# Folding w_phi in quarter-array tiles of 60 by 64

## The chip, the cores and the metric

The kernel runs on one core of one Trainium2 chip. The metric is the time of one execution on the device in microseconds (us); lower is better. The core has five engines with a queue each: TensorE (PE; its weight loads are shown as PEld), VectorE (DVE), ScalarE (ACT), GpSimd (POOL) and SyncE (SP), which issues the DMAs here. PE writes to PSUM banks only; DVE and ACT copy from there.

## The reference

Two layers, each a linear attention with a learned feature map and a dense block with Mish, both on layer-normed rows and added to their input. S = 2048 rows, D = 640, H = 32 heads of 20, F = 1536, all in float32.

```python
def A(x, wqkv, w_phi, wo):
    q, k, v = split(x @ wqkv)                       # B, H, S, 20 each
    pq, pk = q @ w_phi[h], k @ w_phi[h]             # per head, 20 by 20
    phi_q = concat(softmax(pq), softmax(-pq))
    phi_k = concat(softmax(pk), softmax(-pk))
    kv, z = phi_k.T @ v, sum over s of phi_k
    return ((phi_q @ kv) / (phi_q @ z + 1e-6)) @ wo
def B(x, w1, b1, w2): return mish(x @ w1 + b1) @ w2
for _ in range(2):
    x = x + A(layernorm(x), wqkv, w_phi, wo)
    x = x + B(layernorm(x), w1, b1, w2)
```

## The kernel before

**Numbers in two parts.** A matrix product of float32 precision is made of three fp32r products: high by high, high by low, low by high. A weight or an activation is therefore kept as a pair: `hi` is copied by ACT with rounding to fp32r, and `lo` is the difference, made by DVE or POOL. `split` (L141) does it for weights that lie in SBUF, `fold_end` (L272) for products in PSUM, and `Transposed.step` (L316) for transposed rows (`xth`, `xtl`).

**The fold.** Since the features depend on q and k only through q·w_phi and k·w_phi, the kernel multiplies w_phi into the weights of queries and keys once, at the start of the first layer. A softmax does not change when a constant is taken off each head's 20 scores, so one of the 20 columns is subtracted from the other 19 (`shift_phi`, on POOL) and DL = 19 columns a head are kept: 608 in all. The weights of queries and keys come transposed from DRAM (`wqk_t`), in six raw tiles for the queries and six for the keys (`load_raw`). `bd` holds w_phi as blocks along a diagonal: 120 rows, six tiles, 120 columns. `fold_part` multiplies raw tile t (up to 120 rows, six heads) by one of the five 128-column slices k, with f32 operands; an f32 product is recorded twice in the trace. A tile's result is up to 114 columns wide. Three tiles fill one PSUM bank, 342 or 266 columns, and `fold_end` evicts it: one ACT copy to `r2h` (queries) or `r1h` (keys), one DVE subtraction to `r2l` or `r1l`. There are ten evictions for the queries and ten for the keys.

**PSUM.** There are eight banks: two tiles `mm` of two banks each and four tiles `one` of one bank. A tile is handed out again only when its readers are done with it.

**The start.** Under `written()` the order of PE, SP, ACT, DVE and POOL is the order of the code. 30 transposes of the identity come first on PE. SP issues the first 256 rows of x (a block: two tiles of 128 rows), w_phi, the raw tiles of the queries, the values' weights, the raw tiles of the keys and the next block's rows, in this order. On PE follow the first fold (tiles 0 to 2) of slices 0 to 3, the ten transposes of the first block's normed rows `xn`, the first fold of slice 4, the first half of the first queries' projection (`project_half`: 15 products, three per slice), the second folds (tiles 3 to 5) of all five slices, and the second half. On ACT the eviction of slice 0 stands ahead of `xn[0]`. `make_v` splits the values' weights between the evictions of the second folds.

**The first layer's blocks.** Afterwards a scheduler orders PE, ACT, DVE and POOL by its own estimates of time; `tc.issue_after(x)` keeps an instruction behind x. Block 0 goes through `q0 v0 v1 k0 q1 k1`; the digit is the tile of 128 rows. The keys' fold (`fold_phi`) stands in the code ahead of `k0`. `features` turns projected queries or keys into softmax features: eviction by ACT, reduces and subtractions on DVE and POOL (L416 to L419), exp on ACT, a sum, a reciprocal and a product (L425 on DVE, L426 on DVE, L427 on POOL). For keys PE then accumulates the state `kva` (L464: 32 products of 21 by 40 columns a tile). For queries DVE transposes the features (L478) and SP writes them to DRAM in four pieces (`e_d`). `fetch_normed(b + 1)` makes the statistics of the next block: four `bn_stats` and two aggregates on DVE, a power on POOL.

**The rest.** `attend_second` makes the outputs of the attention; its `average` (L686) multiplies features by the state in products of 64 columns of the stationary operand, one for each half of PSUM's partitions. `dense` makes the second part of the layer. The second layer does the same with the folded weights from DRAM (`wp_d`).

## Time and profile before

| | |
|---|---|
| median of 3 runs | 1363.56 us (1362.27 to 1363.75) |
| the profiled execution's own time | 1361.69 us |
| its span, first to last instruction | 1359.7 us |
| busy PE, DVE, ACT, POOL | 1349.6, 1057.4, 576.0, 464.0 us |
| mean granted clock of PE | 0.999 |

The span is what the trace shows; the profiled execution's own time is 2.0 us more. In the rows of the trace a line such as L262 is the line of the kernel, `out<-in` are the names of the tiles that an instruction writes and reads, x is a count, and the text in brackets tells how long the engine was idle in front of it and what ended that. Matmuls are pipelined, so the rows of PE overlap: the distance of two starts is the price of a product, not its own length.

### The profile page before, as it was taken

How to read it: one execution, taken by the hardware profiler on the slowest of the kernel's cores; microseconds unless marked ns; L12 is line 12 of the kernel's file. 1: busy time of each engine (PE TensorE's matmuls, PEld its weight loads, DVE VectorE, ACT ScalarE, POOL GpSimd, SP SyncE). 2: the span in 40 equal slices, each digit the busy share in tenths (PEclk: the TensorE clock that was granted, in tenths of full speed). 3: DMA queues.
4: the chain of work that ended last, by engine and by line, in shares of the span. 5: the costliest groups of instructions: out<-in, count | busy, mean ns of one | idle time of the engine just before them, and what ended most of it. 6: DMA issues, size and time to landing. Idle time of an engine off the chain costs nothing.

```text
span 1359.7 us, 30969 instructions
## 1 busy us (share of the span) xinstructions
PE 1349.6 (99%) x12896; PEld 1338.2 (98%) x12896; DVE 1057.4 (78%) x1799; ACT 576.0 (42%) x967; POOL 464.0 (34%) x417
## 2 busy tenths in 40 slices
PE   9999999999999999999999999999999999999998
PEld 9999999999999999999999999999999999999998
DVE  5888988876687887778769788779668776676775
ACT  4444344322454545445443334332236444444443
POOL 2355644444222222222225555634351211111111
PEclk9999999999999999999999999999999999999999
DMA  9543443797714442244563534559964221233200
GB/s 338 156 103 79 98 96 81 206 287 274 222 40 98 117 117 69 61 106 100 145 209 81 119 79 91 96 120 289 289 246 125 78 72 39 86 98 97 73 26 20
DMA packets 352629, 174.11 MB, mean 128 GB/s; under 512 B 287449, under 2 KB 324041, under 8 KB 352489
## 3 DMA queue, kind: packets, MB, share of 16 engines
q1 hardware_dynamic: 352489, 172.14, 46.7%
q8 instruction: 101, 1.65, 0.5%
q14 instruction: 39, 0.32, 0.1%
HBM read 106.23 MB, written 65.86 MB: 127 GB/s over the span
## 4 chain that ended last, share of the span: by engine, by line
PE 94%; DVE 3%; POOL 1%; ACT 0%; issue 0%; DVEq 0%; POOLq 0%
PE mm L391 25%; PE mm L851 25%; PE one L809 25%; PE one L391 12%; PE mm L686 3%; PE one L325 2%; PE one L464 2%; DVE r L425 1%; DVE m L416 0%; DVE r L419 0%; POOL big L427 0%; DVE big L417 0%; DVE r1l L276 0%; POOL xtl L331 0%; POOL r L427 0%
## 5 line engine op out<-in xcount | busy, mean ns | idle before, releaser
L851 PE MATMUL mm<-r2h,ol 128*128 128x320 f32 x1280 | 304.8, 309 | 0.0
L835 POOL TENSOR_TENSOR ol<-big,ol 128x512 fp32r<-128x512 f32 (+1 forms) x98 | 131.1, 1338 | 477.2 <-ACT ol L834 419.1
L809 PE MATMUL one<-xtl,r1h 128*128 128x256 f32 x960 | 268.2, 279 | 0.0
L809 PE MATMUL one<-xth,r1l 128*128 128x256 f32 x960 | 268.0, 279 | 0.0
L809 PE MATMUL one<-xth,r1h 128*128 128x256 f32 x960 | 265.9, 279 | 0.0
L851 PEld LDWEIGHTS mm<-r2h,ol 128*128 128x128 f32 x1280 | 219.2, 188 | 0.0
L851 PE MATMUL mm<-r2l,ol 128*128 128x320 f32 x640 | 197.3, 309 | 0.0
L391 PE MATMUL mm<-r1h,xth 128*128 128x304 f32 (+1 forms) x600 | 185.1, 309 | 1.5 <-DVE r1l L276 1.5
L391 PE MATMUL mm<-r1l,xth 128*128 128x304 f32 (+1 forms) x600 | 183.8, 306 | 0.0
L391 PE MATMUL mm<-r1h,xtl 128*128 128x304 f32 (+1 forms) x600 | 183.5, 306 | 0.2 <-POOL xtl L331 0.2
L809 PEld LDWEIGHTS one<-xtl,r1h 128*128 128x128 f32 x960 | 180.4, 188 | 0.0
L809 PEld LDWEIGHTS one<-xth,r1l 128*128 128x128 f32 x960 | 180.4, 188 | 0.0
L809 PEld LDWEIGHTS one<-xth,r1h 128*128 128x128 f32 x960 | 179.6, 188 | 0.0
L824 DVE TENSOR_SCALAR big<-big 128x512 f32<-128x512 f32 (+1 forms) x98 | 56.6, 578 | 110.0 <-ACT big L822 109.8
L851 PEld LDWEIGHTS mm<-r2l,ol 128*128 128x128 f32 x640 | 120.2, 188 | 0.0
L834 ACT ACTIVATE ol<-big 128x512 fp32r<-128x512 f32 (+1 forms) x98 | 60.9, 622 | 137.8 <-DVE big L833 137.8
L826 ACT ACTIVATE big<-big,two 128x512 f32<-128x512 f32 (+1 forms) x98 | 70.1, 716 | 116.0 <-DVE big L825 115.9
L822 ACT ACTIVATE big<-one,b1s 128x256 f32<-128x256 f32 x192 | 80.9, 468 | 88.5 <-PE one L809 88.0
L427 POOL TENSOR_TENSOR r<-r,r 128x1280 f32<-128x1280 f32 x32 | 77.2, 2413 | 119.1 <-DVE r L426 101.6
L391 PEld LDWEIGHTS mm<-r1h,xth 128*128 128x128 f32 x600 | 112.8, 188 | 2.6 <-DVE r1l L276 1.7
L391 PEld LDWEIGHTS mm<-r1h,xtl 128*128 128x128 f32 x600 | 112.8, 188 | 0.4 <-POOL xtl L331 0.4
L391 PEld LDWEIGHTS mm<-r1l,xth 128*128 128x128 f32 x600 | 112.8, 188 | 0.1
(142 smaller groups left out, 3118.0 us busy)
## 6 DMA issues: line engine op xcount, KB each, us to landing
e_d<-r SPq DMA_DIRECT2D x128, 160.0 KB, 4.0
big<-e_d SPq DMA_DIRECT2D x32, 640.0 KB, 7.6
x_d<-xt SPq DMA_DIRECT2D x23, 640.0 KB, 3.8
xt<-x_d SPq DMA_DIRECT2D x22, 640.0 KB, 5.5
n_d<-xn SPq DMA_DIRECT2D x168, 80.0 KB, 2.3
xt<-in_x SPq DMA_DIRECT2D x16, 640.0 KB, 4.4
xn<-x_d SPq DMA_DIRECT2D x28, 320.0 KB, 4.4
v<-n_d SPq DMA_DIRECT2D x30, 256.0 KB, 3.1
```

The costliest lines, as they stand in the source:

```text
L325: nc.tensor.transpose(ps[:, c, t * P:(t + 1) * P], self.rows[t][:, (c0 + c) * P:(c0 + c + 1) * P], ident)
L391: nc.tensor.matmul(ps[:, :w], a[:, sl], r, start=(k == 0 and n == 0), stop=(k == KD - 1 and n == 2))
L427: nc.gpsimd.tensor_tensor(eg, eg, r.unsqueeze(2).to_broadcast([P, 2 * H, DH]), op=ALU.mult)
L464: nc.tensor.matmul(kva[32 * j:32 * j + DH + 1, 40 * r:40 * r + 40], v[:, (DH + 1) * h:(DH + 1) * (h + 1)], e[:, 40 * h:40 * h + 40], start ...
L686: nc.tensor.matmul(po[64 * q:64 * q + 64, c, GW * j:GW * j + w], phs[g][:n, s0:s0 + 64], kvb[:n, g, :w], start=True, stop=True)
L809: nc.tensor.matmul(ph[:, j, :], l, r, start=(n == 0), stop=(n == 3 * KD - 1))
L822: exps[0] = nc.scalar.activation(part(ta, 0)[:, j - js.start], ph[:, j, :], AF.Exp, bias=b1s[:, 2 * pr + j:2 * pr + j + 1]).ins
L824: nc.vector.tensor_scalar_min(e, e, E_CAP)
L826: nc.scalar.activation(r, n, AF.Ln, bias=two)
L834: nc.scalar.activation(ah[:, js], n, AF.Copy)
L835: nc.gpsimd.tensor_tensor(al[:, js], n, ah[:, js].bitcast(F32), op=ALU.subtract)
L851: nc.tensor.matmul(pys[t][:, c, :HC], l[:, j, sl], r, start=(f == 0 and n == 0), stop=(f == KF - 1 and n == 2))
```

## The change

Each group of the fold (one raw tile, one slice) is made of four products of 60 (or 64) rows by 64 columns of the raw tile, with 57 columns of w_phi, in place of one of up to 120 rows by 128 columns with 114. Rows 0 to 63 and rows 64 to 123 go to two PSUM banks, the two 64-column halves of a slice to the two halves of a bank's partitions. The sixth tile has only the upper rows: two products. So that a half starts at row 64, a raw tile is loaded from four rows further up, with those rows meeting zeros in `bd`; `bd` is now 128 rows by six tiles of 60 columns, filled with zeros by DVE first. `fold_end` evicts both banks of an `mm` tile in one instruction with a two-part pattern, and two `one` tiles in two instructions; the sixth tile's 38 columns of an `mm` tile take one more.

The order at the start changes too: the first fold begins with three slices, `xn[0]` on ACT and `xn[1]` on DVE stand ahead of all evictions, the folds of slices 3 and 4 follow between the transposes, the first half of the first queries' projection comes behind the second folds of slices 0 and 1, and `make_v` starts one slice later. The keys' fold is in two parts: slices 0 and 1 ahead of `v1`, slices 2 to 4 behind it and ahead of `k0`, each behind the product that PE was given last. The first queries' next steps (`advance`) go behind the last eviction of the keys' fold. The statistics are tied down: those of block 1 behind the last v split, of block 3 behind a reciprocal of block 1, of the others behind the last eviction of the fold.

```diff
         raw = []
         for t in ts:
-            rows = 120 if t < 4 else 80
-            if t < 5:
-                r = wts.tile([P, D], F32, tag=f"r2{'hl'[which]}{5 + t}", name=f"raw{which}{t}")
-            else:
-                r = r2_wide(10 + which, F32)[:, 0]
-
-            n = P if t < 5 else rows
-            c0 = which * D + (t * 120 if t < 5 else D - rows)
-            nc.sync.dma_start(r[:n], wqk_t[c0:c0 + n, :])
-            raw.append((r, rows))
+            r = (wts.tile([P, D], F32, tag=f"r2{'hl'[which]}{5 + t}", name=f"raw{which}{t}") if t < 5 else
+                 r2_wide(10 + which, F32)[:, 0])
+            p0 = 4 if which == t == 0 else 0
+            n = 124 if p0 else P if t < 5 else 64
+            c0 = which * D + (120 * t - 4 if t < 5 else D - 64)
+            if p0:
+                nc.vector.memset(r[:p0], 0.0)
+            nc.sync.dma_start(r[p0:n], wqk_t[c0 + p0:c0 + n, :])
+            raw.append(r)
         return raw
 
-    def fold_part(ps, k, t, bd, raw):
-
-        r, rows = raw[t]
-        heads = rows // DH
-        n = DL * (6 * (t % 3) if t < 5 else 10)
-        nc.tensor.matmul(ps[:, n:n + heads * DL].rearrange("p (j d) -> p j d", d=DL), r[:rows, k * P:(k + 1) * P],
-                         bd[:rows, t, :rows].rearrange("p (j d) -> p j d", d=DH)[:, :, :DL], start=True, stop=True)
+    def load_phi(bd):
+
+        nc.vector.memset(bd, 0.0)
+        for s in range(2):
+            nc.sync.dma_start(bd[4 + 60 * s:64 + 60 * s, :5], phi_bd[60 * s:60 * s + 60, :5, 60 * s:60 * s + 60])
+        nc.sync.dma_start(bd[24:64, 5, :40], phi_bd[:40, 5, :40])
 
...
-    def fold_end(ws, ps, k, c):
-        n0, n1 = (0, 18 * DL) if c == 0 else (18 * DL, QK)
-        hi, lo = ws[k][0][:, n0:n1], ws[k][1][:, n0:n1]
-        nc.scalar.activation(hi, ps[:, :n1 - n0], AF.Copy)
-        nc.vector.tensor_tensor(lo, ps[:, :n1 - n0], hi.bitcast(F32), op=ALU.subtract)
-
-    def fold_phi(ws, bd, raw):
-
-        pss = {}
-        for k, c in ((0, 0), (1, 0), (2, 0), (3, 0), (0, 1), (1, 1), (2, 1), (3, 1), (4, 0), (4, 1)):
-            if c == 0:
-                mm = None if k % 2 else mm_tile()
-                pss[k] = [one_tile(), one_tile()] if k % 2 else [mm[:, 0], mm[:, 1]]
-            ps = pss[k][c]
-            for t in range(3 * c, 3 * c + 3):
-                fold_part(ps, k, t, bd, raw)
-            fold_end(ws, ps, k, c)
+    def pair_banks(single):
+
+        if single:
+            return [one_tile(), one_tile()]
+        mm = mm_tile()
+        return [mm[:, 0], mm[:, 1], mm]
+
+    def fold_part(ps, k, t, t0, bd, raw):
+
+        n = 3 * (t - t0) * DL
+        heads = 3 if t < 5 or len(ps) == 2 else 2
+        for s in range(2 if t < 5 else 1):
+            rows = slice(64 * s, 64 if s == 0 else 124)
+            rhs = bd[rows, t, :heads * DH].rearrange("p (j d) -> p j d", d=DH)[:, :, :DL]
+            for q in range(2):
+                last_product[0] = nc.tensor.matmul(
+                    ps[s][64 * q:64 * q + 64, n:n + heads * DL].rearrange("p (j d) -> p j d", d=DL),
+                    raw[t][rows, k * P + 64 * q:k * P + 64 * q + 64], rhs, start=True, stop=True).ins
+
+    def fold_end(ws, ps, k, t0, t1):
+
+        n = min(t1, 5) - t0
+        w = 3 * DL
+        c0 = 2 * t0 * w
+
+        outs = []
+        if len(ps) > 2:
+            out = [x[:, c0:c0 + 2 * n * w].rearrange("p (t s d) -> p s t d", t=n, s=2) for x in ws[k]]
+            outs.append((ps[2][:, :, :n * w].rearrange("p s (t d) -> p s t d", t=n), *out))
+            if t1 > 5:
+                outs.append((ps[0][:, n * w:n * w + 2 * DL], *(x[:, 10 * w:QK] for x in ws[k])))
+        else:
+            for s in range(2):
+                m = t1 - t0 if s == 0 else n
+                out = [x[:, c0 + s * w:c0 + (2 * m - 1 + s) * w] for x in ws[k]]
+                out = [bass.AP(tensor=x.tensor, offset=x.offset, ap=[x.ap[0], [2 * w, m], [1, w]]) for x in out]
+                outs.append((ps[s][:, :m * w].rearrange("p (t d) -> p t d", t=m), *out))
+        for src, hi, lo in outs:
+            last_copy[0] = nc.scalar.activation(hi, src, AF.Copy).ins
+            last_fold[0] = nc.vector.tensor_tensor(lo, src, hi.bitcast(F32), op=ALU.subtract).ins
+
+    def fold_phi(ws, bd, raw, ks):
+
+        for k in ks:
+            ps = pair_banks(k == 3)
+            for t in range(6):
+                fold_part(ps, k, t, 0, bd, raw)
+            fold_end(ws, ps, k, 0, 6)
...
             xt = fetch(x_src, b) if b > 1 else early
-            norm_scale(b, [norm_stats(t, xt) for t in range(BT)])
+            with tc.issue_after(last_split[0] if b == 1 else early_recip[0] if b == 3 else last_fold[0]):
+                norm_scale(b, [norm_stats(t, xt) for t in range(BT)])
...
-                bd = big_tile()[:120, :720].rearrange("p (t c) -> p t c", t=6)
-                nc.sync.dma_start(bd[:, :3], phi_bd[:, :3])
+                bd = big_tile()[:, :360].rearrange("p (t c) -> p t c", t=6)
+                load_phi(bd)
...
-                shift_phi(bd, slice(3, 5))
-                shift_phi(bd, 5)
+                shift_phi(bd, slice(3, 6))
...
                 q_ws = [r2_pair(k) for k in range(KD)]
-                mm = [mm_tile(), mm_tile()]
-                pcs = [mm[0][:, 0], mm[0][:, 1], mm[1][:, 0], mm[1][:, 1], one_tile()]
+                def fold(ps, k, t0):
+                    for t in range(t0, t0 + 3):
+                        fold_part(ps, k, t, t0, bd, raw_q)
+
+                def make_v(k):
+                    split(kv_ws[k][0][:, D:2 * D], kv_ws[k][1][:, D:2 * D], raw_v[k])
+
+                pcs = [pair_banks(k == 2) for k in range(3)]
                 for t in range(3):
-                    for k in range(KD - 1):
-                        fold_part(pcs[k], k, t, bd, raw_q)
-                fold_end(q_ws, pcs[0], 0, 0)
+                    for k in range(3):
+                        fold_part(pcs[k], k, t, 0, bd, raw_q)
                 xn = [row_tile() for _ in range(BT)]
                 act(xn[0], xt[:, 0, :], AF.Identity, bias=stats[:, 0, 1, 0:1], scale=stats[:, 0, 0, 0:1])
                 nc.vector.tensor_scalar(xn[1], xt[:, 1, :], stats[:, 0, 0, 1:2], stats[:, 0, 1, 1:2],
                                         op0=ALU.mult, op1=ALU.add)
-                fold_end(q_ws, pcs[1], 1, 0)
-                fold_end(q_ws, pcs[2], 2, 0)
+                fold_end(q_ws, pcs[0], 0, 0, 3)
                 nxt = Transposed(xn)
                 nxt.step()
-                fold_end(q_ws, pcs[3], 3, 0)
+                pcs.append(pair_banks(False))
+                fold(pcs[3], 3, 0)
+                fold_end(q_ws, pcs[1], 1, 0, 3)
+                fold_end(q_ws, pcs[2], 2, 0, 3)
                 nxt.step()
-                for t in range(3):
-                    fold_part(pcs[4], 4, t, bd, raw_q)
+                pcs.append(pair_banks(True))
+                fold(pcs[4], 4, 0)
+                fold_end(q_ws, pcs[3], 3, 0, 3)
                 nxt.step()
-                fold_end(q_ws, pcs[4], 4, 0)
+                fold_end(q_ws, pcs[4], 4, 0, 3)
                 mm = mm_tile()
                 q0 = [mm[:, 0], mm[:, 1], mm]
-                project_half(q0[0], nxt, 0, q_ws, 0, 0, w=QC)
-
-                def make_v(k):
-                    split(kv_ws[k][0][:, D:2 * D], kv_ws[k][1][:, D:2 * D], raw_v[k])
-
                 for k in range(KD):
-                    ps = one_tile()
-                    for t in range(3, 6):
-                        fold_part(ps, k, t, bd, raw_q)
-                    fold_end(q_ws, ps, k, 1)
-                    if k > 0:
-                        make_v(k - 1)
+                    ps = pair_banks(k in (1, 2, 4))
+                    fold(ps, k, 3)
+                    fold_end(q_ws, ps, k, 3, 6)
+                    if k == 1:
+                        project_half(q0[0], nxt, 0, q_ws, 0, 0, w=QC)
+                    elif k > 1:
+                        make_v(k - 2)
                 project_half(q0[1], nxt, 0, q_ws, 0, 1, w=QC)
+                make_v(KD - 2)
                 make_v(KD - 1)
...
                 i = b * BT + t
+                if b == 0 and layer == 0 and n in (2, 3):
+                    with tc.issue_after(last_product[0]):
+                        fold_phi(kv_ws, bd, raw, range(2) if n == 2 else range(2, KD))
                 if b == 0 and n == (1 if layer else 3):
-                    if layer == 0:
-                        fold_phi(kv_ws, bd, raw)
...
-                if b == NB - 1 and n == 3:
+                if b == 0 and not layer:
+                    with tc.issue_after(last_product[0]):
+                        next(g)
+                    if n == 3:
+                        with tc.issue_after(last_fold[0]), tc.issue_after(last_copy[0]):
+                            advance()
+                    elif n != 2:
+                        advance()
...
+                if b == 1 and n == 0:
+                    early_recip[0] = last_recip[0]
```

21 lines of the change are left out of this document (9 added, 12 removed).

## The prediction

> **What bounds the kernel now.** I read the page first, then busy time by stretches, then the timeline of TensorE (PE) up to 43 us, then the groups of the first 43 us by shape.
>
> ```profile
> span 1359.7 us, 30969 instructions
> ...
> PE 1349.6 (99%) x12896; PEld 1338.2 (98%) x12896; DVE 1057.4 (78%) x1799; ACT 576.0 (42%) x967; POOL 464.0 (34%) x417
> ```
> ```profile
> 0.00:20.00 20.00, 17.75 (x127) 17.19 (x128) 10.00 (x27) 8.95 (x19) 3.76 (x16) 1.00 0.94 317
> 20.00:40.00 20.00, 17.46 (x133) 17.07 (x133) 16.20 (x41) 10.05 (x22) 6.56 (x9) 1.00 1.00 361
> 40.00:60.00 20.00, 20.00 (x147) 20.00 (x146) 15.23 (x26) 6.20 (x9) 3.97 (x8) 1.00 0.52 132
> 60.00:80.00 20.00, 20.00 (x260) 19.51 (x259) 19.99 (x26) 8.98 (x12) 10.06 (x7) 1.00 0.34 72
> 80.00:100.00 20.00, 20.00 (x257) 19.51 (x256) 15.79 (x22) 9.69 (x15) 12.48 (x13) 1.00 0.52 133
> ```
>
> After the stretch come its length and then the busy time of PE, PEld, DVE, ACT, POOL, the granted clock, the DMA share and GB/s. PE is the bound, and the 10 us in which it is idle (1359.7 less 1349.6) lie, as far as these stretches reach, in the first 40 us: 20 − 17.75 and 20 − 17.46. From 40 us on it has no gap. DVE is full from 60 to 80 us, though, so PE can be moved forward there only as far as DVE follows.
>
> The change touches only the work up to the first keys; the built programs' orders agree on every engine again from about the third block of rows on (near 100 us). So the question is how much earlier PE reaches its gapless part, and whether that part stays gapless.
>
> ```profile
> 1.15 0.47 SPq L503 DMA_DIRECT2D big<-in_phi_bd  x1
> 1.68 1.30 SPq L253 DMA_DIRECT2D raw<-in_wqk_t  x3
> ...
> 7.13 2.83 PE L262 MATMUL mm<-big,raw 120*128 120x114 f32 x24
> ...
> 8.12 0.23 DVE L307 SCALAR_TENSOR_TENSOR stats<-mv,stats 128x1 f32<-128x1 f32 x2 [1.10 <-POOL stats L305]
> ...
> 9.90 0.91 ACT L131 ACTIVATE xn<-xt,stats 128x640 f32<-128x640 f32 x1
> 10.87 1.25 PE L325 MATMUL one<-ident,xn 128*128 128x128 f32 x8 [0.91 <-ACT xn L131]
> 12.74 0.39 PE L391 MATMUL mm<-r2h,xth 128*128 128x304 f32 x1
> ...
> 30.15 0.82 PE L262 MATMUL one<-big,raw 120*128 120x114 f32 x6
> 30.80 0.83 PE L262 MATMUL mm<-big,raw 120*128 120x114 f32 x6
> ...
> 35.34 0.67 PE L262 MATMUL mm<-big,raw 120*128 120x114 f32 x4 [1.05 <-DVE r1l L276]
> 39.47 0.41 PE L391 MATMUL mm<-r1h,xth 128*128 128x304 f32 x1 [1.49 <-DVE r1l L276]
> ...
> 41.98 0.39 PE L391 MATMUL mm<-r1l,xth 128*128 128x304 f32 x1
> 42.20 0.31 PE L391 MATMUL mm<-r1h,xtl 128*128 128x304 f32 x1
> ```
>
> The columns are start, length, engine, line, operation and, in brackets, the idle time in front. Three gaps of PE stand here: 0.91 us, in which the transposes wait for the norm of the first rows, and 1.05 and 1.49 us, in which the keys' fold waits for DVE's evictions: 3.45 us. The last two rows end the first half of the first keys' projection (15 products) at 42.4 us. That is my checkpoint: both programs have then done the same PE work, all ten transposes of the second block included.
>
> **Term 1: the fold on PE.** I call a group one raw tile times one 128-column slice: 6 tiles × 5 slices × 2 (queries, keys) = 60. Before, a group is one product, recorded twice (f32). Three start at 30.15 and the next three at 30.80: 0.22 us a group, 13.2 us in all. After, a group is four products of 64 by 64 and 57 columns (two for the sixth tile), one in each quarter of the array. The trace has no products in row halves; it has them in column parts:
>
> ```profile
> 251.64 0.30 PE L391 MATMUL one<-r2l,xth 128*128 128x304 f32 x1
> 251.78 0.30 PE L391 MATMUL one<-r2h,xtl 128*128 128x304 f32 x1
> 252.01 1.39 PE L686 MATMUL mm<-kvb,big 120*64 120x63 f32 x40
> ...
> 253.32 1.36 PE L686 MATMUL mm<-kvb,big 120*64 120x63 f32 x40
> ...
> 65.54 0.83 PE L464 MATMUL one<-big,v 128*21 128x40 f32 x64
> ```
>
> 304 columns take 0.14 us, 0.46 ns a column. An f32 group of 114 columns at 0.22 us is about 4 × 114 × 0.46 = 0.21, so f32 streams four times. A pair of 64-wide products (L686) takes 0.12 us: 22 of them, 44 records, from 252.01 to 253.32 give 1.31/11. One alone would need 4 × 63 × 0.46 = 0.116, so the two column halves run at once. If row halves do too, a group costs 4 × 57 × 0.46 = 0.105 to 0.12, by the nearest row; I take 0.112: 60 × 0.112 = 6.7 us, 6.5 us less. If row halves follow each other, it is 0.22 in 50 groups. If all four follow each other, 0.42. PE also changes its shape of product some ten times more: 251.78 to 252.01 is 0.23 us against 0.14 inside a run, so 0.1 each, 1 us.
>
> The Trainium skill (TensorE: Matmul & The Clock Gate, Part 1) says that starts of matmuls are never under about 25 ns apart however few the columns. By it a group's eight records would take 0.2 us and the fold would gain nearly nothing. The L464 row speaks against this: 64 records in 0.83 us are 13 ns each.
>
> **Term 2: the first norm.** In front of xn on ACT stands one eviction today. It goes behind, so xn runs from 8.35 (8.12 + 0.23) to 9.3. On PE nine groups (three slices instead of four) stand in front: 7.13 + 1.0, or, when the third raw tile lands late, 9.0 + 0.35. Before, its groups start after eight others, at 7.13 + 8 × 0.236 = 9.0, with no gap, so it lands by then. SP's queue now has three pieces of w_phi in front of the raw tiles instead of one, behind a fill of bd on DVE: two issues of up to 0.47 and the fill put the tiles' issue at most 1.2 us behind 1.68. I cost that at nothing, since the data queues behind the rows of x and xn at 9.3 covers a landing up to 9.0; without that cover it costs up to 1.2 (in the range). The transposes start at 9.35 instead of 10.87.
>
> **Term 3: evictions of the queries.**
>
> ```profile
> L276 DVE TENSOR_TENSOR r2l<-mm,r2h 128x342 fp32r<-128x342 f32 x4 | 2.0, 510 | 1.8 <-ACT r2h L275 1.7
> ...
> L331 DVE TENSOR_TENSOR xtl<-one,xth 128x512 fp32r<-128x512 f32 x3 | 2.1, 685 | 0.2 <-ACT xth L131 0.2
> L275 ACT ACTIVATE r2h<-mm 128x342 fp32r<-128x342 f32 x4 | 1.7, 453 | 7.6 <-PE mm L262 7.6
> L131 ACT ACTIVATE xth<-one 128x512 fp32r<-128x512 f32 x2 | 1.2, 602 | 0.2 <-PE one L325 0.2
> L142 ACT ACTIVATE r1h<-v 128x640 fp32r<-128x640 f32 x2 | 1.5, 752 | 0.0
> L143 DVE TENSOR_TENSOR r1l<-v,r1h 128x640 fp32r<-128x640 f32 x2 | 1.6, 816 | 0.0
> ```
>
> The same 608 columns a slice are copied, in 17 pairs of ACT and DVE instructions instead of 10. On DVE 170 columns more (342 to 512) take 0.175 us more, so 342 columns are 0.35 us and the fixed part is 0.16: seven new pieces are 1.1 us on each engine, not on the path where PE or the landing is late. PE's queue is in order: slice 1's second fold (in front of the first projection) now waits for the third transposed pair's DVE subtract. From xth at 10.1, ACT runs 2 × 0.60 + 0.4 and five evictions of 0.45 to 0.6, 0.1 overlapped each, to 13.2; DVE frees the bank at 13.6; the first query half starts at 14.0 (12.74 today) and ends at 16.2 (15 × 0.144), but two of five second folds are behind it. Nine groups follow, to 17.3. The second half then waits for slice 4: on ACT from 16.6, four pieces of 0.25, two v splits of 0.75 that are queued between, one of 0.35, and 1.2 in which a 38-column piece waits for DVE, where a v split of 0.82 stands in front: 16.6 + 4.05 = 20.7, and DVE 0.8 more. So it ends at 21.9, after 2.4 us of waiting.
>
> Then PE runs the first values (30 × 0.145 = 4.35, by 0.46 a column) to 26.25, twelve groups of the keys to 27.8, the second values to 32.15, eighteen groups to 34.25, four transposes to 34.8. In the keys' first half, slice 4 waits for DVE: fold end 34.25, ACT's queue to 35.9, DVE 36.6; its three products end at 37.1. Waits named here: 3.4 before 14.0, 2.4, and 0.2.
>
> Sum at the checkpoint: 42.4 − 37.1 = **5.3 us earlier**. The keys' evictions in between hide under the second values (4.35 us over 2 × 1.3 of ACT).
>
> **Term 4: what follows on DVE.** The change puts work of the first queries behind the keys' fold:
>
> ```profile
> 32.96 1.49 DVE L425 TENSOR_REDUCE r<-r 128x64 f32<-128x1280 f32 x1 [1.48 <-ACT r L134]
> 36.31 0.54 DVE L426 RECIPROCAL r<-r 128x64 f32<-128x64 f32 x1
> 40.54 1.46 DVE L478 STREAM_TRANSPOSE r<-r 128x1280 f32<-128x1280 f32 x1
> ...
> 45.35 0.82 DVE L416 TENSOR_REDUCE m<-big 128x32 f32<-128x640 f32 x1 [2.28 <-ACT big L134]
> 58.77 2.37 POOL L427 TENSOR_TENSOR big<-big,r 128x1280 f32<-128x1280 f32 x1 [6.96 <-DVE r L426]
> ...
> 87.71 2.37 POOL L427 TENSOR_TENSOR big<-big,r 128x1280 f32<-128x1280 f32 x1
> 90.80 0.83 PE L464 MATMUL one<-big,v 128*21 128x40 f32 x64
> ```
>
> 3.5 us (1.49 + 0.54 + 1.46) now follow the first keys' reduce, which itself comes 4.5 us earlier (it waits for statistics and POOL's power to about 40.8). DVE has 4.8 us idle from 40 to 60, 2.3 of them in front of 45.35, so some 2 us to catch up: its lead is 4.5 − 3.5 + 2 = 3 us against PE's 5.3. What PE's kva products need is ready ahead of time by 4.4 us at 65.54 (58.77 + 2.37) but by 0.7 at 90.80 (87.71 + 2.37). So up to 5.3 − 3 − 0.7 = 1.6 us are given back; without that cover, all 2.3. I take 1.3, as the order there was also rebuilt. The statistics of block 3, put behind a reciprocal, move within this same DVE time.
>
> **Sum.** 5.3 − 1.3 = 4.0 us: span 1355.7, profiled time 1361.69 − 4.0 = 1357.7. The three runs' median, 1363.56, is 1.87 above the profiled one; against it, **1359.6**.
>
> **Rivals.** *B: row halves take turns.* For it: no row shows row halves at once; a group then costs what it does today. 50 × 0.11 = 5.5 us come back, some 1 us of it under the waits before 14.0 and 17.3 to 21.9: 5.3 − 4.5 = 0.8 earlier, and DVE keeps pace: 1362.8, between 1361.5 and 1365. *C: the quarters do not overlap at all* (slower). Four products of 0.105 give 0.42 a group, 50 × 0.42 + 10 × 0.21 = 23.1 against 13.2, 9.9 us more; with the 6.5 not gained and waits of 3 us that hide a part, the checkpoint comes 16.4 − 5.3 − 3 = 8 us later: 1371. It decides from about 0.3 us a group. Against it: L686's pair. *D: DVE is the bound to 100 us.* For it: 19.99 of 20 us from 60 to 80. If the rebuilt order spends no idle time of DVE, its lead is 1 us, and PE gains 1 + 0.7: 1361.9. *E: nothing changes in effect* can't be: the orders differ on every engine to 100 us.
>
> **Chances.** A (0.112 a group, the sum above) 0.66; within it the ends are group prices of 0.105 and 0.12, half or one and a half times the 6 us of waits (±3), 0 to 2.3 given back: 1356.5 to 1363. B 0.13, D 0.13, C 0.08. The range 1356.5 to 1365.5 holds A, B and D but for their tails. 0.2% is 2.7 us, about what a measurement can tell here. Faster by more than that: most of A, 0.58. Within: a fifth of A, most of B and D, 0.28. Slower: C, B's and A's tails, 0.14.
>
> **What would show it.** Fold rows of PE in 64-row tiles at about 0.11 us a group; no idle PE over 1 us between 22 and 37 us; the L686 and L464 rows unchanged; the first keys' half done near 37 us. Wrong, if a group takes 0.2 us or more, if the queries' second half ends after 25 us, or if PE has gaps in front of kva's products between 60 and 100 us.

## The result

The changed kernel takes 1367.89 us (median of 6 runs, 1367.52 to 1369.49); the kernel before, run beside it, 1362.88 (6 runs, 1362.27 to 1363.75). The ratio is 1.0038 (95% interval 1.0025 to 1.0051): 5.0 us slower, where 1359.6 was forecast. The profiled execution after took 1367.52 us with a span of 1365.7. Its page and its busy times by stretches, in the order of columns that the prediction names:

```profile
span 1365.7 us, 31618 instructions
...
PE 1349.5 (99%) x13216; PEld 1335.4 (98%) x13216; DVE 1063.1 (78%) x1807; ACT 576.9 (42%) x974; POOL 463.2 (34%) x416
```
```profile
0.00:20.00 20.00, 16.18 (x284) 14.03 (x284) 10.90 (x31) 7.91 (x21) 3.06 (x15) 1.00 0.95 305
20.00:40.00 20.00, 18.97 (x309) 17.77 (x309) 13.53 (x31) 11.39 (x27) 3.37 (x7) 0.91 0.99 362
40.00:60.00 20.00, 20.00 (x145) 20.00 (x144) 17.31 (x30) 7.08 (x9) 5.67 (x6) 1.00 0.47 127
60.00:80.00 20.00, 19.67 (x255) 18.88 (x253) 20.00 (x30) 8.25 (x11) 10.94 (x13) 1.00 0.27 60
80.00:100.00 20.00, 15.81 (x216) 15.29 (x217) 16.16 (x22) 7.74 (x12) 10.85 (x9) 0.91 0.58 134
```

The stretch of 80 to 100 us, gapless before, now has 4.2 us without PE, and two stretches show a granted clock of 0.91 where it was 1.00. Busy PE time did not fall, though the fold did: with each record counted up to the next one's start, the fold's products take 9.0 us of PE instead of 13.5, but the projections take 4.2 us more, of which about 3.2 lie in the two stretches at half clock that are shown below. The timeline after, at the places that count:

```profile
9.77 0.66 PE L354 MATMUL one<-ident,xn 128*128 128x128 f32 x4
10.68 0.57 PE L285 MATMUL mm<-big,raw 64*64 64x57 f32 x24 [0.26 <-DVE r2l L309]
...
22.11 0.41 PE L420 MATMUL mm<-r2l,xth 128*128 128x304 f32 x1 [0.53 <-DVE r2l L309]
...
42.76 0.68 ACT L135 ACTIVATE big<-mm 128x608 f32<-128x608 f32 x1 [3.30 <-PE mm L420]
...
58.79 1.60 DVE L324 BATCH_NORM_STATS2 bn<-xt 128x6 f32<-128x320 f32 x4
...
67.50 2.82 POOL L456 TENSOR_TENSOR r<-r,r 128x1280 f32<-128x1280 f32 x1 [0.28 <-DVE r L455]
...
68.02 2.39 DVE L336 SCALAR_TENSOR_TENSOR stats<-mv,stats 128x1 f32<-128x1 f32 x2
70.33 1.66 DVE L324 BATCH_NORM_STATS2 bn<-xt 128x6 f32<-128x320 f32 x4
...
74.61 1.45 DVE L508 STREAM_TRANSPOSE r<-r 128x1280 f32<-128x1280 f32 x1
76.09 3.32 SPq L511 DMA_DIRECT2D e_d<-r  x4
...
83.46 0.68 ACT L135 ACTIVATE r<-mm 128x608 f32<-128x608 f32 x1 [8.96 <-DMA e_d<-r]
84.19 0.62 PE L420 MATMUL mm<-r1h,xth 128*128 128x304 f32 x1 [4.53 <-ACT r L135]
```

Read from below: PE waits 4.53 us because it needs an `mm` bank; ACT, which would empty it, waits for the query tile (there are two, `i % 2`), whose old contents are still being written out by four DMAs; these were issued at 76.09, since DVE transposed the tile (the second transposition) only at 74.61. The rows that match before, the last two being the eviction at 83.46 and the product at 84.19:

```profile
44.64 0.68 ACT L134 ACTIVATE big<-mm 128x608 f32<-128x608 f32 x1 [2.03 <-PE mm L391]
...
69.83 1.45 DVE L478 STREAM_TRANSPOSE r<-r 128x1280 f32<-128x1280 f32 x1
...
77.70 0.68 ACT L134 ACTIVATE r<-mm 128x608 f32<-128x608 f32 x1 [3.96 <-DMA e_d<-r]
...
81.36 0.30 PE L391 MATMUL mm<-r1h,xth 128*128 128x304 f32 x1
```

So PE came to the first keys' eviction 1.9 us earlier than before (42.76 against 44.64), and DVE came to the second transposition 4.8 us later. The granted clock has stretches of its own, 3.41 us long, of which four rows say what is needed (same columns):

```profile
19.01:22.42 3.41, 2.25 (x12) 1.48 (x11) 2.71 (x7) 2.48 (x7) 0.00 (x0) 1.00 1.07 299
22.42:25.83 3.41, 3.41 (x15) 3.41 (x14) 3.41 (x8) 1.30 (x3) 0.16 (x1) 0.50 1.03 382
...
80.45:83.86 3.41, 0.00 (x0) 0.00 (x0) 2.12 (x6) 0.40 (x1) 0.54 (x2) 1.00 0.31 48
83.86:87.27 3.41, 3.08 (x12) 3.03 (x12) 2.98 (x4) 3.04 (x6) 3.41 (x2) 0.50 0.09 24
```

In these rows a stretch in which PE does little is followed by one at half clock, which costs up to 1.7 us, half its length, where PE is busy in it. The sum: −1.9 (lead at the first keys, with the first half-clock stretch already in it) + 4.5 + 1.7 = +4.3 at 95 us; another 1.9 us is lost between 199 and 409 us; the difference of the spans is 6.0.

### The profile page after: what moved, and what is told of

Its sections match the earlier page's. It is cut to its first block, busy times and chain, and to the rows that moved or that the text cites. A ratio compares the mean times of both kernels' runs of the same rounds, so it can differ in the third digit from the quotient of the medians.

```text
span 1365.7 us, 31618 instructions
## 1 busy us (share of the span) xinstructions
PE 1349.5 (99%) x13216; PEld 1335.4 (98%) x13216; DVE 1063.1 (78%) x1807; ACT 576.9 (42%) x974; POOL 463.2 (34%) x416
## 4 chain that ended last, share of the span: by engine, by line
PE 90%; DVE 4%; DMA 2%; POOL 1%; issue 1%; SPq 1%; ACT 1%; DVEq 0%; ACTq 0%; POOLq 0%
PE mm L891 25%; PE one L849 25%; PE mm L420 23%; PE one L420 12%; PE mm L726 3%; PE one L354 2%; PE one L494 1%; DMA e_d<-r 1%; DVE m L445 1%; DVE r L454 1%; DVE r L448 1%; DVE big L446 0%; DMA big<-e_d 0%; DMA raw<-in_w 0%; SPq L511 0%
```

## The experiments

Every kernel was timed in five rounds beside the kernel before. In the diffs a line ` ...` stands where lines are left out. The table gathers what the traces say; the second transposition is the start of DVE's transposition of the second query tile. A lead is the start of one of ACT's evictions of projected features or dense outputs, less the start of the same one before (44.64, 90.91, 199.23 and 409.04 us); minus is earlier.

| kernel | at 44.6 | at 90.9 | at 199 | at 409 | second transposition | median us | ratio to before |
|---|---|---|---|---|---|---|---|
| before | 0 | 0 | 0 | 0 | 69.83 | | 1 |
| changed | −1.9 | +4.3 | +4.3 | +6.3 | 74.61 | 1367.9 | 1.0038 [1.0025, 1.0051] |
| f1 third buffer | −2.8 | +4.6 | +4.6 | +6.5 | 74.50 | 1368.1 | 1.0042 [1.0030, 1.0054] |
| c2 f1, gap filled | −2.7 | +3.4 | +3.4 | +5.3 | 74.54 | 1366.6 | 1.0026 [1.0017, 1.0035] |
| e7 before, statistics held back | −2.5 | 0.0 | 0.0 | +0.2 | 71.75 | 1364.7 | 1.0009 [0.9999, 1.0019] |
| p1 e7, third buffer | −2.3 | +3.7 | +3.7 | +4.5 | 71.93 | 1367.9 | 1.0037 [1.0024, 1.0049] |
| g1 statistics earlier | −2.2 | +3.4 | +3.4 | +4.3 | 74.15 | 1367.2 | 1.0020 [1.0011, 1.0028] |
| n1 statistics left out | −3.1 | −1.1 | −0.6 | +1.4 | 70.48 | 1363.3 | 1.0002 [0.9993, 1.0011] |
| n2 before, the same left out | −2.1 | −2.2 | −2.1 | −2.0 | 67.68 | 1362.6 | 0.9990 [0.9981, 0.9999] |
| k1 queries' steps at once | +0.4 | +4.7 | +4.7 | +6.7 | 74.64 | 1368.5 | 1.0039 [1.0026, 1.0052] |
| k2 k1 and g1 | +0.2 | +0.2 | +1.5 | +4.1 | 70.03 | 1365.0 | 1.0010 [1.0001, 1.0019] |

**Statistics not held back at all** (e1).

```diff
-            with tc.issue_after(last_split[0] if b == 1 else early_recip[0] if b == 3 else last_fold[0]):
-                norm_scale(b, [norm_stats(t, xt) for t in range(BT)])
+            norm_scale(b, [norm_stats(t, xt) for t in range(BT)])
```

> The changed kernel with one part of the change undone: the statistics of blocks 1 to 3 are no longer held back behind the last split, the last fold and an early reciprocal. Theory T (backlog and buffer): the 4.5 us in which TensorE waits at 84.2 us come from VectorE, whose work between 40 and 80 us got longer by statistics that were put there; the stream transposition of the second query tile (74.6 us, before 69.8) and its four writes end late, and the third query evictions wait for that buffer. Undone, the transposition comes back to 70 to 72 us, the gap falls below 1 us, and the half-clock stretch behind it (83.9 to 87.3) goes too: 4.5 + 1.7 less, 0.5 to 1 us lost where statistics now stand between the queries' evictions: about 1362.5 (1361 to 1364.5). Rival S (the backlog is the first queries' own sum, reciprocal and transposition, which the quarter fold puts behind the keys' fold; the statistics only fill idle time): a gap of over 3 us stays, 1366 to 1369. Rival Q (the head gained nothing that could be given back): the first keys' evictions start at 44 us or later and the time is above 1363.5 even without the gap.

Measured: 1383.5 us, ratio 1.0147 [1.0133, 1.0160]. The first row is the answer:

```profile
23.99 0.49 DVE L324 BATCH_NORM_STATS2 bn<-xt 128x6 f32<-128x320 f32 x1 [8.17 <-DMA xt<-in_x]
...
24.78 0.47 PE L285 MATMUL one<-big,raw 64*64 64x57 f32 x4 [5.05 <-DVE r2l L309]
```

Left free, the statistics of block 1 were put ahead of the queries' evictions in DVE's queue, and DVE stood 8.17 us waiting for rows that landed at 24. All else moved 15 us. The run says why the statistics of block 1 are held back. The gap itself stayed (4.42 us, up to 100.70, with half clock behind it), which is the sign of rival S, but the times of T and S both missed, and Q's bounds were passed by the stall alone. With so much shifted the run does not decide between T and S; k1, g1 and k2 below do.

**A third query tile** (f1), and the clock's part at 20 us (d1, d2).

```diff
     def query_tile(i):
-        return r2_wide(10 + i % 2, F32).rearrange("p s d -> p (s d)")
+        return r2_wide(7 if i == 3 else 10 + i % 2, F32).rearrange("p s d -> p (s d)")
 ...
```

> The changed kernel with one more buffer: the fourth query tile (the first to wait for a write-out) lies in the space of two raw tiles that are done by then, instead of in the second query tile's buffer; nothing is computed differently and TensorE's order is the same. Theory T: TensorE's gap of 4.5 us at 84.2 goes, and the half clock behind it: 1367.9 - 4.5 - 1.7 = 1361.7 if nothing is late behind it (1361 to 1363.5). Rival V (VectorE itself is late, the buffer is only the first place where it shows): a gap of 2 to 4 us comes some microseconds later, in front of the next evictions or of the key-value products at 88 to 95 us, and the time is 1365 to 1368. Rival Q: as long as before the change at best, 1363 or more.

Measured: 1368.14 us. The gap at 84.19 went and a longer one came 1.5 us later:

```profile
83.31 2.36 POOL L461 TENSOR_TENSOR big<-big,r 128x1280 f32<-128x1280 f32 x1
...
85.72 1.40 PE L499 MATMUL one<-big,v 128*21 128x40 f32 x64 [5.32 <-POOL big L461]
```
```profile
79.93:83.35 3.42, 0.48 (x4) 0.23 (x2) 3.42 (x7) 0.00 (x0) 1.39 (x3) 1.00 0.45 69
```

That is rival V, with a gap larger than its 2 to 4 us: the third group of key-value products needs POOL's product, which needs DVE's reciprocal (82.09). DVE is full in the whole row from 79.93 to 83.35. The buffer was only the first place at which DVE's lateness showed. Two half-clock stretches follow here, 83.35 to 90.18.

```diff
+                for _ in range(13):
+                    nc.tensor.matmul(q0[1][:, :QC], nxt.hs[0][:, :P], q_ws[0][0][:, QC:2 * QC], start=True, stop=True)
                 project_half(q0[1], nxt, 0, q_ws, 0, 1, w=QC)
```

> The changed kernel with 13 idle products (the first product of the second query half, started anew each time, so its last start is the only one that counts) in front of the second query half, where TensorE waits for evictions anyway. Theory H (TensorE's clock falls to half for 3.4 us at 22.4 us because its stream was thin from 18 to 22.4 us): with the products TensorE streams without a break there, the granted clock stays at 1.00 from 20 to 40 us, the first values take 4.35 us instead of 6.0, and the first keys' evictions start at about 41.1 us instead of 42.8. The end is hardly earlier, since the query tile's write-out is late as before and TensorE waits 6 us for it instead of 4.5: 1366.5 to 1368.5. Rival P (products in quarters of the array, or the dense products behind them, lower the clock): the half-clock stretch stays, and so do 42.8 us and 1367.9.

> Both edits at once: the 13 idle products in front of the second query half and the buffer of its own for the fourth query tile. If theories T and H both hold, their gains add up, because no wait at 84 us eats what the clock gives: 1367.9 - 4.5 - 1.7 - 1.7 = 1360.0 (1359.3 to 1362). If VectorE is late by itself (rival V), what the clock gives is given back: as the kernel with the buffer alone, within 0.5 us. If the clock does not come from the thin stream (rival P), as the buffer alone too, with the half-clock stretch at 22 us still there.

Measured: 1370.72 (ratio 1.0060 [1.0046, 1.0074]) and 1372.38 (1.0071 [1.0054, 1.0088]). In both the clock stayed at 1.00 up to 40 us, but in f1, without the idle products, it did too, so these two runs don't show that the products did it. The gain did not come through: PE then stood idle for 1.60 us (2.05 in d2) in front of transposes at 40 us, with nothing in the trace that it waited for, and in d2 a half-clock stretch followed that. The forecasts missed; the two runs settle little.

**The wait at 84 us filled with idle work** (c1, c2), in the kernel with the third buffer.

```diff
+            if i == 2 and not layer:      # c1: without "and not layer"
+                idle = one_tile()
+                with tc.issue_after(last_product[0]):
+                    for _ in range(32):
+                        last_idle = nc.tensor.matmul(idle[:, :QC], xts.hs[0][:, :P], kv_ws[0][0][:, :QC],
+                                                     start=True, stop=True).ins
 ...
```

> The kernel with the buffer of its own for the fourth query tile (1368.1, TensorE waits 5.3 us at 80.4 to 85.7, then half clock for 6.8 us), with 32 idle products (4.5 us, into a bank that nothing reads) put into that wait. Theory H (the wait itself makes the clock fall, and that is a second cost): no half clock from 80 to 95 us, though TensorE does no useful work earlier: 1368.1 - 3.4 = 1364.7 (1364 to 1366). Rival P (what comes behind the wait lowers the clock): half clock as before, 1368 or more.

> The kernel with the buffer of its own for the fourth query tile, and the 32 idle products in its wait, now only in the first layer (in the run before they were issued in the second layer too, where no wait hides them, and cost 4.1 us near 750 us). Theory H: no half clock from 80 to 95 us, so 1.6 to 3.4 us less than the kernel with the buffer alone (1368.1): 1364.7 to 1366.5. Rival P (the fall of the clock costs nothing, since TensorE then waits less later): 1367.5 or more.

Measured: 1370.97 (c1) and 1366.60 (c2). c1 issued the idle products in the second layer as well, where nothing hides them (lead +4.9 at 725 us, +8.9 at 757). c2 has them once: no half clock from 80 to 95 us, PE waits 1.43 us at 86.50 for the same product of POOL, and the median is 1.5 us below f1's, just short of the 1.6 to 3.4 of theory H; the intervals of the two ratios overlap, but in the traces c2 is 1.2 us ahead of f1 at 90.9 us. So the half clock is a cost of its own, on top of the wait, of some 1.2 to 1.5 us here.

**One part of the change alone, on the kernel before** (e7), and with a third buffer (p1): the statistics held back, whole-tile fold.

```diff
-            norm_scale(b, [norm_stats(t, xt) for t in range(BT)])
+            with tc.issue_after(last_split[0] if b == 1 else early_recip[0] if b == 3 else last_fold[0]):
+                norm_scale(b, [norm_stats(t, xt) for t in range(BT)])
 ...
```

> The kernel before with one part of the change alone: the statistics of blocks 1 to 3 held back as the change does it (behind the last split, the last eviction of the keys' fold, the reciprocal of the first keys of block 1); the fold stays in whole tiles. Theory T: VectorE gets late by 3 us or more in front of the second and third key-value products, TensorE, which has 0.7 us to spare there, waits 1 to 4 us between 75 and 92 us, possibly with a half-clock stretch behind it: 1364 to 1369. Rival V: the statistics find idle time of VectorE, TensorE has no new gap: 1362 to 1363.5.

> The kernel before with the statistics held back as the change does it (alone: 1364.7, lead of 2.5 us at the first keys, taken back by a wait of 2.2 us at 81 us for the second query tile's buffer), and the fourth query tile in a buffer of its own. Theory D (VectorE takes the lead back, the buffer is only the first place where it shows): a wait of 1 to 3 us comes at the third key-value products instead, 1363 to 1365.5. Rival L (the buffer alone takes it back): no wait over 0.7 us from 60 to 100 us, 1361 to 1362.

Measured: 1364.65 (e7, which cannot be told from the kernel before) and 1367.90 (p1).

```profile
42.13 0.68 ACT L134 ACTIVATE big<-mm 128x608 f32<-128x608 f32 x1 [2.03 <-PE mm L391]
...
71.75 1.50 DVE L479 STREAM_TRANSPOSE r<-r 128x1280 f32<-128x1280 f32 x1
...
81.23 0.41 PE L391 MATMUL mm<-r1h,xth 128*128 128x304 f32 x1 [2.22 <-ACT r L134]
```
```profile
82.53 0.41 PE L397 MATMUL mm<-r1h,xth 128*128 128x304 f32 x1 [1.66 <-ACT xth L134]
...
84.60 1.40 PE L471 MATMUL one<-big,v 128*21 128x40 f32 x64 [1.52 <-POOL big L433]
```
```profile
80.01:83.42 3.41, 1.41 (x9) 0.91 (x7) 2.60 (x6) 2.48 (x5) 2.55 (x3) 1.00 0.08 26
83.42:86.83 3.41, 2.23 (x67) 2.12 (x68) 3.41 (x3) 0.40 (x1) 3.41 (x2) 0.50 0.27 101
```

The first fence is e7, the other two p1. Moving the statistics away from the keys' fold alone brings the first keys 2.5 us forward: more than the whole change in its profiled run (1.9). The lead is then waited away to 0.0 by 91 us, without half clock. In p1 a lead of 2.3 is waited away in two gaps; the first and the start of the second fall into one stretch of the clock (PE busy 1.41 of 3.41), two half-clock stretches follow, and the kernel is as slow as the changed one, without a single quarter product in it. Theory T's range held e7, D's did not hold p1: its waits were forecast, the clock was not.

**Key-value products later in PE's order** (h7 with the third buffer, h8 without).

```diff
-            if i % BT == 0 and BT < i < NT - BT:
+            if i % BT == 0 and BT <= i < NT - BT or i == 3:
                 yield
 ...
+                        with tc.issue_after(last_product[0]) if i in (2, 3) else nullcontext():
```

> The changed kernel with the buffer of its own for the fourth query tile and, besides, the third and fourth groups of key-value products put later in TensorE's order: the third behind 48 instead of 16 projection products after the second, the fourth behind 46 more. The computation is the same. Theory R (TensorE reaches the third group 5.3 us before VectorE and GpSimd have its operand, which is ready at 85.7 us; it has other work it could do first; the half clock behind the wait is a second cost): no gap over 1 us between 78 and 100 us, no half-clock stretch, and 1368.1 - 5.3 - 3.4 = 1359.4 (1358.8 to 1361.5). Rival V (VectorE is the bound up to 100 us, so that TensorE must wait as long somewhere): gaps of 3 us or more in sum come further behind, 1363.5 or more.

> As the run before this one, but with the two query tiles of the changed kernel: only the third and fourth groups of key-value products are put later. Theory R: the third query evictions still wait for the write-out of the second tile, so the gap of about 4.5 us at 84 us and the half clock behind it stay: 1366 to 1368.5. Rival O (the order of the key-value products alone is the cost, the buffer's wait would be hidden by the work in front): no gap over 2 us, 1359.5 to 1362.

Measured: 1369.94 (1.0042 [1.0030, 1.0054]) and 1369.65 (1.0049 [1.0034, 1.0064]). Theory R fell:

```profile
83.25 1.27 ACT L135 ACTIVATE big<-big 128x1280 f32<-128x1280 f32 x1 [8.57 <-DVE big L453]
...
84.84 0.42 PE L425 MATMUL mm<-r1h,xth 128*128 128x304 f32 x1 [4.40 <-ACT xth L135]
```

With the key-value products out of the way PE ran on and met the next thing that DVE had not done: ACT stood 8.57 us for a DVE subtraction, and the transposed rows (`xth`) that PE needs were behind that in its queue. h8 waits 5.01 us at 83.72 for the query tile, as forecast, but two half-clock stretches follow and its time lies above the forecast.

**Statistics one place earlier** (g1).

```diff
-            with tc.issue_after(last_split[0] if b == 1 else early_recip[0] if b == 3 else last_fold[0]):
+            with tc.issue_after(last_split[0] if b < 3 else last_fold[0]):
```

> The changed kernel with the statistics of blocks 2 and 3 put one place earlier each: block 2's behind the last split of the values (its rows land at 25.6 us, VectorE is idle there), block 3's behind the last eviction of the keys' fold (landed at 36.0). Theory T (late statistics are what makes VectorE late): 1.75 us of VectorE leave the stretch up to 42 us and as much the stretch from 58 to 63, the stream transposition of the second query tile starts at 71 to 72.5 us instead of 74.6, and the gap at 84 us falls to 1 to 2 us, too little for a half clock: 1362.5 to 1365. Rival V (VectorE would be as late without them, by the first queries' own steps and by its port conflicts with GpSimd): a gap of 4 us or more and a half-clock stretch stay, 1367 to 1369.

Measured: 1367.23. The transposition came at 74.15, 0.5 us earlier and not 2 to 3; the gap is 3.73 and the half clock stayed. Theory T by itself falls. g1's rows show where the room went: DVE is idle 1.00 us at 63.05, waiting for ACT, and 0.61 us at 71.11, waiting for the rows of block 4, whose statistics still stand ahead of the second transposition. A DVE subtraction of 0.8 us took 2.99 at 67.05, beside a POOL product, but the changed kernel loses as much in its row of 68.02.

**VectorE relieved** (n1 the changed kernel, n2 the kernel before, whose edit is shown).

```diff
-            norm_scale(b, [norm_stats(t, xt) for t in range(BT)])
+            if not 2 <= b <= 4:
+                norm_scale(b, [norm_stats(t, xt) for t in range(BT)])
 ...
```

> The changed kernel with part of the work left out: the statistics of blocks 2, 3 and 4 (5.3 us of VectorE) are not computed, block 1's are used instead. Theory D (VectorE sets the pace up to about 90 us; TensorE's wait at 84 us and the half clock behind it are VectorE's lateness): the second transposition starts at 67 to 70 us instead of 74.6, no gap of TensorE over 1 us and no half clock between 60 and 100 us, 1367.9 - 4.5 - 1.7 = 1361.7 (1360.5 to 1363.5). Rival B (the buffers and GpSimd's products hold TensorE, not VectorE's load): a gap over 2 us stays, 1365 or more.

> The kernel before with the same part left out (the statistics of blocks 2, 3 and 4). Theory D: the first keys' evictions start 2.5 us earlier, as they did where only the statistics were held back, and now nothing takes it back: 1363.6 - 2.5 = 1361.1 (1360.3 to 1362). With the run before this one it says what the fold in quarters is worth where VectorE has room: forecast there 0.5 to 1.5 us better than this, and no difference if the fold in quarters gains nothing. Rival B: no gain, 1362.8 or more.

Measured: 1363.30 and 1362.64. In the fence n1 comes first, in the next n2:

```profile
70.48 1.50 DVE L510 STREAM_TRANSPOSE r<-r 128x1280 f32<-128x1280 f32 x1
...
80.20 0.41 PE L421 MATMUL mm<-r1h,xth 128*128 128x304 f32 x1 [1.70 <-ACT r L135]
```
```profile
42.50 0.68 ACT L134 ACTIVATE big<-mm 128x608 f32<-128x608 f32 x1 [2.03 <-PE mm L392]
...
88.76 0.68 ACT L134 ACTIVATE big<-mm 128x608 f32<-128x608 f32 x1 [2.36 <-PE mm L392]
```

With the statistics of three blocks taken off DVE (and their share of POOL with them), the changed kernel gets 4.6 us faster: its lead of 3.1 is cut to 1.1, most of it by a wait of 1.70 us, with no half clock. The kernel before keeps a lead of 2.1 at 199 us and 2.0 at 409. n1's time lies in D's range but its transposition (70.48) and its gap are later and larger than forecast; n2's median is 1.5 us above the forecast, its profiled run (1360.06) below. Theory D holds in its main point: DVE's load between 40 and 85 us takes the lead back. And with room on DVE the fold in quarters is no better than the whole-tile fold (1.0002 [0.9993, 1.0011] against 0.9990 [0.9981, 0.9999]), where 0.5 to 1.5 us better was forecast. Its added evictions and the first queries' steps, which still lie late in n1, are the likely reasons; no run parts them.

**The first queries' steps back in their old place** (k1), with g1 (k2), with the third buffer (k4), with the transposition put later (m1), and that with the statistics left out (o1). The lines on `transpose` are in m1 and o1 alone.

```diff
-                nc.vector.transpose(e, e)
+                with (tc.issue_after(last_fold[0]) if i == 0 and not layer else nullcontext()):
+                    nc.vector.transpose(e, e)
 ...
-                    if n == 3:
-                        with tc.issue_after(last_fold[0]), tc.issue_after(last_copy[0]):
-                            advance()
-                    elif n != 2:
-                        advance()
+                    advance()
```

> The changed kernel with the first queries' steps moved on at every step of block 0 again (the change skips one and holds the next behind the keys' fold); fold, evictions and statistics stay as changed. Theory S (the first queries' sum, reciprocal and transposition, 3.5 us of VectorE that now lie in the stretch where VectorE has no idle time, make it late): they run between the evictions of the keys' fold instead, the keys' first evictions start up to 1 us later than 42.8, the second transposition starts at 71 to 72.5 us instead of 74.6, TensorE waits 2 us or less near 84 us without a half clock: 1362 to 1364.5. Rival T (statistics alone): the transposition stays later than 73.5 us, a gap of 4 us and a half clock stay, 1366 to 1369.

> As the run before this one, and the statistics of blocks 2 and 3 one place earlier as well: VectorE then has nothing in its full stretch that the kernel before did not have there. Theory D (VectorE is what sets the pace up to about 90 us, and TensorE keeps only as much of its lead as VectorE gains): the second transposition starts at 70 us or earlier, TensorE has no gap over 1 us from 60 to 100 us, no half clock, and the time is 1361 to 1363. Rival Q (the fold in quarters costs VectorE more by its added evictions than it gains TensorE): a gap of 1 to 3 us stays, 1363.5 to 1366.

> As the run before this one, with the buffer of its own for the fourth query tile. If the write-out of the second tile is still the wait that ends last there, 0.5 to 2 us less than without the buffer (1360 to 1362.5); if VectorE's operands are (theory D), the same within 0.5 us.

> The kernel with the first queries' steps moved on at every step and the statistics of blocks 2 and 3 one place earlier (1365.0), and besides the first stream transposition put behind the last eviction of the keys' fold: there it stood in front of that eviction and waited 1.7 us for GpSimd. The gap of 2.4 us at 38.2 us falls below 1 us and the half clock behind it goes, so the first keys' evictions start near 42 us instead of 44.9. Theory D: TensorE's lead of 2 to 3 us is taken back between 70 and 90 us (gaps of 1.5 to 2.5 us in sum, too little in one place for a half clock): 1364 to 1365.5. Rival L (the lead was lost only there): no gap from 60 to 100 us, 1361 to 1362.5.

> The run before this one with the statistics of blocks 2, 3 and 4 left out (block 1's are used). Theory D: the lead of 2 to 3 us stays to 130 us, no gap over 1 us from 40 to 130 us: 1360 to 1362. Rival B: a gap over 1.5 us between 60 and 100 us, 1363 or more.

Measured: 1368.52, 1364.97, 1364.84 (1.0013 [1.0005, 1.0022]), 1365.05 (1.0019 [1.0010, 1.0028]) and 1364.79 (1.0012 [1.0003, 1.0021]). k2's rows:

```profile
34.58 1.49 DVE L454 TENSOR_REDUCE r<-r 128x64 f32<-128x1280 f32 x1 [1.44 <-ACT r L135]
...
38.16 0.38 PE L420 MATMUL mm<-r1h,xth 128*128 128x304 f32 x1 [2.44 <-DVE r1l L309]
...
70.03 1.45 DVE L508 STREAM_TRANSPOSE r<-r 128x1280 f32<-128x1280 f32 x1
```
```profile
35.04:38.45 3.41, 0.97 (x10) 0.74 (x7) 2.98 (x6) 1.92 (x6) 1.12 (x1) 1.00 1.01 371
38.45:41.86 3.41, 3.41 (x16) 3.38 (x15) 2.14 (x3) 0.00 (x0) 1.41 (x3) 0.50 1.04 402
```

With both undone DVE keeps to its times of before (70.03 against 69.83), PE's order is practically that of before from the first key-value products on, and no gap is left from 60 to 100 us. But the lead is gone already: the sum and the reciprocal stand among the evictions of the keys' fold, PE waits 2.44 us for those, and half clock follows. So the 3.5 us of DVE are paid in front of 38 us (k2) or behind 74 us (changed kernel); none of the runs found a third place. m1 was meant to remove the 2.44 and did not (2.43): the transposition was not what stood in the way.

Four of these kernels make a square that the table does not show. From the first reduce of the first keys to the second transposition DVE takes 24.5 us in the kernel before (45.35 to 69.83). It takes 24.3 with both parts undone (k2, 45.77 to 70.03), 28.4 with the statistics alone held back (k1, 46.20 to 74.64), 31.0 with the steps late and the statistics of blocks 2 and 3 early (g1, 43.13 to 74.15; those of block 4 stand ahead of the transposition there) and 31.1 with both (changed, 43.47 to 74.61). So the two costs do not add up: either one brings the transposition to 74 us, and undoing one of them, as k1 and g1 do, brings it forward by 0.5 us at most.

Of the forecasts, theory S missed in k1; rival T held in the transposition, the half clock and the time, but the gap is 2.48 us and not 4, since PE had lost its lead to 2.73 us at 38. k2 did between 60 and 100 us what theory D forecast, but is 2 us above its range: it has no lead left to keep, and in its profiled run it loses another 3.9 us behind 91 us. m1's time was in D's range, by another way than forecast. o1 has no gap over 1 us from 41 to 130 us, as forecast, but lost its lead at 40 like k2 (2.72 us) and had half clock from 15.53 to 18.94. k4 equals k2 in the median, as theory D says. No version is faster than the kernel before by more than a measurement can tell; only n2, which leaves work out, is below it at all.

## Why the prediction was wrong

**Term 1** was right in the price of a group. The 24 records from 10.68 are three groups; of their 0.57 us the last record's own length is 0.22, so a group takes 0.35/3 = 0.117 us, forecast 0.112. Rivals B and C are out. The whole fold takes 9.0 us of PE against 13.5, so it saves 4.5, where the term had 6.5 less 1 for changes between kinds of product. A group of four products is eight records, so that is 15 ns a record. The rule that starts of matmuls are never under about 25 ns apart, which the Trainium skill states (TensorE: Matmul & The Clock Gate, Part 1), does not hold for the records of products in quarters of the array here. Counted by products, each recorded twice, it is 29 ns, which the rule would allow. **Term 2** was right within half a microsecond: the transposes start at 9.77, forecast 9.35; PE had waited 0.27 us for a raw tile, twice.

**Term 3**, the checkpoint: forecast 37.1, measured 40.5 (12 of the 15 products from 37.62, then six transposes, then three more), so 1.9 us earlier than before and not 5.3. Of the 3.4 us between, 0.6 are the second query half (the values start at 22.54, forecast 21.9); 1.6 are the half-clock stretch, which lay on the first values (22.54 to 28.52, forecast 4.35 us); 0.6 are six transposes ahead of the last three products, which the sum had not counted; the last 0.6 are spread over the changes between kinds of product. In the runs of the same fold where that stretch was at full clock and PE had no other new gap (f1, h7, h8, n1, c1, c2) the first keys came 2.7 to 3.4 us earlier. The term left out was the clock: the waits of 2.4 us were counted as waits, not as what slows the products behind them.

**Term 4** is the step that failed. It had the right engine, and its rule was sound: what is given back is PE's lead, less DVE's, less the room that was there. Wrong was DVE's lead, forecast "4.5 − 3.5 + 2 = 3 us" and measured as −4.8, the lateness of the second transposition. The rows of DVE from the first reduce of the first keys to that transposition say why:

```profile
43.47 1.54 DVE L445 TENSOR_REDUCE m<-big 128x32 f32<-128x640 f32 x2 [0.26 <-ACT big L135]
```

That reduce came 1.9 us earlier (45.35 before), not 4.5. The first queries' steps take 3.3 us there, as forecast (3.5). The statistics, which the term put at nothing ("move within this same DVE time"), take 3.4: two blocks' now lie in this stretch (58.79 and 70.33), where before there were none. Another 0.8, net, goes to rows that stand while POOL works, and 0.8 of idle time is used up, not 2: 1.9 − 3.3 − 3.4 − 0.8 + 0.8 = −4.8. The stretch grew by 6.7 us in all; the held-back statistics alone do most of that, since in e7 it is 4.4 us longer than before.

With the measured shifts the term's rule gives the gap. Before, ACT's eviction into the query tile started at 77.70 and the product that needs its bank at 81.36; PE can follow 0.7 us behind the eviction's start (84.19 less 83.46), so the room was 2.9 us. After, the eviction came 5.8 us later (83.46) and PE 1.9 earlier: 5.8 + 1.9 − 2.9 = 4.8, measured 4.53. The same working gives 2.4 for e7, measured 2.22, and 1.9 for n1, measured 1.70. What the term lacked altogether is the clock: the gap of 4.53 us was followed by a stretch at half clock. Rival D named the right bound, but it priced the gain at 1.7 us where DVE allowed none. The place, too, was not named: the buffers of the query tiles (two) came ahead of the key-value products in the sum of waits; f1 shows that either would have done it.

What stays open is the loss of 1.9 us between 199 and 409 us. Kernels with the quarter fold lose 0.9 to 2.6 there (d2 more), mostly in gaps of 0.5 to 1.2 us near 260 and 323 us; e7 and n2 lose 0.2, p1 0.8. The trace puts them down to loads of `e_d`, to rows from DVE, or to nothing; no run was made for it.

## What to carry to other kernels

Where PE is 99% busy, ask which engine would be next with no idle time, and count that engine's work over the whole stretch up to the point where the two meet: a lead of PE is worth only what the follower can match. An edit that brings PE forward by putting the follower's work off does not gain the difference; it makes a wait that grows with both shifts. Work that is held back has to be counted at the place where it then lies. And waits are dear out of proportion once they leave PE little work in one stretch of the clock: the same microseconds cost less when they are spread over several stretches (e7) than when they meet in one (p1).

## What the runs showed of the hardware

The granted clock goes by fixed stretches of 3.41 us. In these traces each stretch at full clock with under 1.42 us of PE records, up to the span's last microseconds, was followed by one at half clock; stretches with 1.56 us or more were not (e7, from 77.41: 1.60, and clock 1.00 behind it), with four exceptions, among them 19.01 to 22.42 above (2.25 us of records, but only twelve products of 0.14 us). What tells these four apart is open. Full clock did not always come back after one stretch: a half-clock stretch with 2.67 us of PE records or less was followed by another (p1, from 83.42: 2.23), one with 2.84 or more by full clock (changed kernel, from 83.86: 3.08). The Trainium skill (TensorE: Matmul & The Clock Gate, Part 1) describes such a free-running window of 3413 ns and half clock after an idle one. The length agrees with the rows; that the window must be idle does not: 1.41 us of work in 3.41 (p1) were too little. Where a wait falls in the stretches decides: the 2.22 us in e7 cost nothing more, the 1.66 and 1.52 us in p1 brought two stretches at half clock.

Two small DVE instructions, 0.23 us together at 42.98, took 2.39 us at 68.02; the first of them ended at 70.33, where POOL's product of 67.50 ended (70.32). The Trainium skill (SBUF — State Buffer, SBUF: two separate sides) says that DVE and GpSimd share a pair of ports under an exclusive lock, also for a DVE instruction with two inputs in SBUF; this row agrees, and so does g1's subtraction of 2.99 us. In a stretch where DVE is the bound, POOL's products are not free.
